# Gated linear attention and a multiplicative FFN in one kernel: another order in the steps that split x, and earlier loads of x

## Chip, cores and metric

The kernel runs on one core of a Trainium2 chip. The metric is the device time of one execution in microseconds (us). Before the change it is 479.17 us, the median of 6 runs (478.79 to 479.78).

## What is computed

```python
for t in range(S):                                   # B=4, H=8, S=768, D=48
    state = alpha[t][..., None] * state + outer(k[t], v[t])   # per batch and head
    y[t] = q[t] @ state
x = y.transpose(0, 2, 1, 3).reshape(B * S, H * D)    # 3072 x 384
out = ((x @ w1) * (x @ w2)) @ w3 @ w_out             # d_ff = 1024, d_model = 384
```

All activations are fp32. The four weights reach the kernel as 64-bit floats, read as pairs of 32-bit words, so each weight has to be converted to fp32 on the chip first.

## The kernel before

**The recurrence as chunks.** The sequence of each batch is cut into 6 chunks of 128 positions, 24 chunks in all. The main loop (L583) has one step per chunk. Step n does on TensorE (PE), in this order: `attend_state(n-1)` (L369, queries times the carried state), `scores(n)` (L349, keys times queries), `transposed(n+1)` (L309, transposes of the decayed q and k), `attend(n-1)` (L375, values times masked scores), `outer(n)` (L321, the new state), then a few pieces of the FFN's first half (L405), with `decays(n+3)` (L271 or L274, cumulative sums of the logarithms of alpha) among them. The first step of a batch has no state to carry, so L369 is missing in steps 7, 13 and 19.

**What the other engines do for it.** VectorE (DVE) masks the scores (`ms`, L352, two instructions for each chunk), multiplies q and k by their decays (L287), adds up the state (L329, L331), and takes part in all splits and conversions. ScalarE (ACT) copies the transposes out of PSUM (`qkT`, L311, two), copies the attention's output (`x`, L379, two), and does logarithms and exponentials (L256, L260, L277, L278). All PSUM tiles come from one pool of 8 banks in turn: a matmul that opens a bank waits for the instruction that read what was in it before.

**x through DRAM.** `attend` leaves its output x in a buffer of two; `store()` at the head of the next step sends it to the DRAM tensor `xd[g]` (L246). A group g is 3 chunks, 384 tokens. `load_x(g)` (L391) reads it back transposed into `xT`, of which there is one buffer, and `split_x(g)` (L393) splits it into the three parts of `x3`: ACT computes a rounded high part (L397), DVE the remainder (L398) and a third part that corrects the rounding (L399). FFN products (L405, fp32r) use all three. `x3` has one buffer in this half of the kernel, and `xT`'s next load waits for L399 of the split before.

**Which steps split x.** `begin` (L581) maps steps 4, 8, 12, 16, 20 to groups 0 to 4. At such a step the group's load is issued, after `logs`; two steps later, in steps 6, 10, 14, 18 and 22, `split_x` is called after `scores` and `transposed`, and the group's tiles are put into `fill`, from which `run` takes pieces (none in steps 6, 10, 14, 18 and 22, three, three and two in the steps after each). Groups 0 to 3 do 4 of the 8 tiles there, group 4 all 8, so the second half of w1 and w2 is first needed for group 4's later tiles, after the main loop.

**Weight conversion.** A weight block is one load (L189) and a generator: L197, L198, L201, L202 in its first stage, L204, L205, L207 in the second, L214 (ACT) in the third, L216 and L217 (DVE) in the last. `convert(1)` runs one stage. In the later steps it is called once after the split's place, and once more at the end of every third step.

**Who decides the order.** Each engine executes its own list in order. The Tile scheduler makes these lists from the traced program; `tc.issue_after(ins)` holds what is traced in the block behind `ins` on the same engine. `after_marks(...)` (L108) applies it to instructions remembered in `mark`: `("ms", n)` is the second mask, `("qkT", n)` the second copy of the transposes. SyncE (SP) issues nearly all DMAs of the main loop in one in-order queue: for each step x's store, then v, alpha, k and q of later chunks, a weight block, the store of an FFN tile (`abd`, L480). GpSimd (POOL) issues the small DMAs of the decays and, after the main loop, the later loads of x.

**After the main loop** come the FFN's other tiles (L405 with w12), the product w3 times w_out (L405 with wo), and the last projection (L405 with w3o).

Of the kernel before, what the change touches and what calls it, by code (L numbers as in the profile page):

```python
# [10 lines left out]
FP32 = mybir.dt.float32  # L11
# [5 lines left out]
ALU = mybir.AluOpType  # L17
# [3 lines left out]
P = 4096.0  # L21
# [27 lines left out]
def kernel(  # L49
# [12 lines left out]
    nc = tc.nc  # L62
# [43 lines left out]
    st, mark = {}, {}  # L106

    def after_marks(*names):  # L108
        stack = ExitStack()
        for x in names:  # L110
            stack.enter_context(tc.issue_after(mark[x]))
        return stack
# [16 lines left out]
    def load_a(n):  # L129
        if n < N:  # L130
            st["a", n] = inp.tile([C, H, D], FP32, tag="ac", name="ac")
            nc.sync.dma_start(out=st["a", n], in_=rows(alpha, n))

    def load_kq(n):
        if n >= N:
            return
        st["kq", n] = inp.tile([C, 2, H, D], FP32, tag="kq", name="kq")
        nc.sync.dma_start(out=st["kq", n][:, 0], in_=rows(k, n))
        nc.sync.dma_start(out=st["kq", n][:, 1], in_=rows(q, n))  # L139

    def load_v(n):
        if n < N:
            st["v", n] = vs[n % len(vs)]
            nc.sync.dma_start(out=st["v", n][:, :, 0:D], in_=rows(v, n))
# [81 lines left out]
    def convert(steps, ahead=3):  # L226

        for _ in range(steps):
            fetch(ahead)
            if not begun:  # L230
                return
            x = begun.popleft()
            try:
                next(x)
                begun.appendleft(x)
            except StopIteration:
                pass
# [4 lines left out]
    def store():  # L242

        while later:
            dst, src = later.popleft()
            nc.sync.dma_start(out=dst, in_=src)  # L246
# [4 lines left out]
    def logs(n):  # L251
        if n >= N:
            return
        a = st.pop(("a", n)).rearrange("p h d -> p (h d)")
        la = st["la", n] = work.tile([C, DM], FP32, tag="la", name="la")
        nc.scalar.activation(la, a, AF.Ln)  # L256
        if n >= LATE:

            t = st["la", n] = work.tile([C, 2, DM], FP32R, tag="la2", name="la2", bufs=1)
            nc.scalar.copy(t[:, 0], la)  # L260
            nc.vector.tensor_sub(t[:, 1], la, t[:, 0].bitcast(FP32))
        if n in ends:
            nc.gpsimd.dma_start(out=ends[n][2:3], in_=a[0:1])

    def decays(n):
        if n >= N:
            return
        lc = bank()[:, 0:DM]
        la = st.pop(("la", n))
        if n < LATE:  # L270
            nc.tensor.matmul(lc, utri if n % 2 else after, la, start=True, stop=True)  # L271
        else:
            for i in range(2):
                nc.tensor.matmul(lc, sums[:, n % 2], la[:, i], start=(i == 0), stop=(i == 1))  # L274

        e = st["e", n] = work.tile([C, 2, DM], FP32, tag="e", name="e", bufs=3)
        nc.scalar.activation(e[:, 0], lc, AF.Exp, scale=-1.0)  # L277
        mark["e", n] = nc.scalar.activation(e[:, 1], lc, AF.Exp).ins  # L278
        if n in ends:
            nc.gpsimd.dma_start(out=ends[n][0:1], in_=e[0:1, 0])  # L280
        if n + 1 in ends:
            nc.gpsimd.dma_start(out=ends[n + 1][1:2], in_=e[C - 1:C, 1])
        load_ends(n)
# [14 lines left out]
    def transposed(n):  # L298
        if n >= N:
            return  # L300
        qk = qks[n % 3]
        qkT = work.tile([C, 2, NP, C], FP32, tag="qkT", name="qkT")

        tp = [bank().rearrange("p (i j c) -> p i j c", i=2, j=NP) for _ in range(2)]
        for i in range(2):
            for j in range(NP):
                for half in range(2):
                    s = ds(DP * half, DP)
                    nc.tensor.transpose(tp[half][:, i, j, :], qk[s, i, 2 * j:2 * j + 2, :], ident[s, s])  # L309
        for half in range(2):  # L310
            mark["qkT", n] = nc.scalar.copy(qkT[:, :, :, ds(DP * half, DP)], tp[half]).ins  # L311
        st["qkT", n] = qkT
# [30 lines left out]
    def scores(n):  # L343
        qkT = st["qkT", n]
        sc = [bank().rearrange("p (j c) -> p j c", j=NP) for _ in range(2)]
        for j in range(NP):
            for i in range(2):
                r = ds(DP * i, D)
                nc.tensor.matmul(sc[i][:, j, :], qkT[r, 0, j, :], qkT[r, 1, j, :], start=True, stop=True)  # L349
        ms = work.tile([C, 2, NP, C], FP32, tag="ms", name="ms")  # L350
        for i in range(2):
            masked = nc.vector.tensor_tensor(ms[:, i].bitcast(I32), sc[i].bitcast(I32), keep_bc, op=ALU.bitwise_and)  # L352
        ends_of_part1[0] = mark["ms", n] = masked.ins
        st["ms", n] = ms
# [3 lines left out]
    def attend_state(n):  # L358
        qkT = st.pop(("qkT", n))

        y = [bank()[:, 0:HP * C].rearrange("p (j c) -> p j c", c=C) for _ in range(2)]
        st["y", n] = y, [(half * HP + j, i, y[i][ds(DP * half, DP), j, :])
                         for j in range(HP) for i in range(2) for half in range(2)]
        if n % NCH:
            for j, i, to in st["y", n][1]:
                r = ds(DP * i, D)
                nc.tensor.matmul(to, Ts[n % 2][r, j, :], qkT[r, 1, j, :],  # L369
                                 start=(j % HP == 0), stop=False, skip_group_check=True)  # L370
# [18 lines left out]
    def load_x(g, queue=nc.sync):  # L389
        st["xT", g] = xp.tile([C, KM, TG], FP32, tag="xT", name="xT")  # L390
        queue.dma_start(out=st["xT", g], in_=xd[g].rearrange("(k p) t -> p k t", p=C))  # L391

    def split_x(g, i):  # L393
        x = st.pop(("xT", g))
        t = tr[i].tile([C, 3, KM, TG], FP32R, tag="x3", name="x3")
        st["x3", g] = t
        nc.scalar.activation(t[:, 0], x, AF.Copy, scale=1.0 - 2.0 ** -13)  # L397
        nc.vector.tensor_sub(t[:, 1], x, t[:, 0].bitcast(FP32))  # L398
        nc.vector.scalar_tensor_tensor(t[:, 2], t[:, 0].bitcast(FP32), -1.0 - 1.0 / P, x,  # L399
                                       op0=ALU.mult, op1=ALU.add)  # L400

    def products(p, w, x, parts, n, start, stop):
        for part in parts:
# [70 lines left out]
    def gate(g, f):  # L474
        yield from (late_gate if late else early_gate)(g, f)
# [73 lines left out]
    def run(pieces):  # L549

        for _ in range(pieces):
            if not fill:
                return
            try:
                next(fill[0])
            except StopIteration:
                fill.popleft()
# [21 lines left out]


    begin = {4 + 4 * g: (g, range(FH if g < 4 else KF)) for g in range(5)}  # L581

    for n in range(N + 1):  # L583
        store()
        load_v(n + AHEAD - 1)
        load_a(n + 5)
        load_kq(n + AHEAD)
        if n:
            attend_state(n - 1)
        if n < N:  # L590
            scores(n)
        transposed(n + 1)
        if n - 2 in begin:
            g, tiles = begin[n - 2]
            split_x(g, 0)
            fill.extend(gate(g, f) for f in tiles)
        pieces = (0, 3, 3, 2)[(n - 6) % 4] if n > 5 else 0
        if n == 0:
            with after_marks(("qkT", 0)):
                logs(2)  # L600
            decays(2)
            with after_marks(("e", 2)):
                logs(3)
        early = n < 7
        behind = after_marks(("qkT", n + 1), ("qk", n + 1)) if early else ExitStack()
        if n < N - 2:
            with behind:
                convert(2 if n == 0 else 1, 2 if n == 0 else 3)
        advance(n)
        if n:  # L610
            attend(n - 1)
        outer(n)
        run(pieces > 0)
        if early:
            with after_marks(("qkT", n + 1), ("qk", n + 1)):
                convert(1)
        with after_marks(*[("ms", n)] * (n < 3)):
            decayed(n + 2)
        logs(n + 4)
        if n in begin:  # L620
            load_x(begin[n][0])
        convert(early and n > 2)
        run(pieces > 1)
        decays(n + 3)
        if n < N - 2:
            convert(early or n % 3 == 0)
        run(pieces > 2)
        if n == N - 3:
            while begun:
                convert(1)  # L630
            weights.extend(load_out(j) for j in range(KF))
            fetch(4)
# [91 lines left out]
```

## Time and profile before

| what | value |
|---|---|
| median of 6 runs | 479.17 us |
| the profiled execution | 478.79 us, span 477.0 us |
| busy: PE, DVE, ACT, POOL | 457.9, 359.6, 279.3, 73.4 us |
| granted PE clock, 60 to 187 us | 1.00 |
| 57 to 187 us: busy PE, DVE, ACT | 126.05, 110.88, 84.63 us of 130 |
| 57 to 187 us: mean share of the 16 DMA engines | 0.95, at 210 GB/s |

In this execution, by PE's first instruction, step 7 begins at 57.5 us, step 11 at 89.5, step 15 at 118.3, step 19 at 149.3, step 23 at 177.2, and the main loop has ended on PE at about 187. A row of the timeline gives the start, the duration, the engine, the line, what is written from what, and in brackets how long the engine was idle before it and what ended that. Matmuls are pipelined, so PE counts as busy while it streams; the weight loads (PEld) show the short waits better. Durations on one engine overlap by some 0.08 us, so that two masks of 0.68 us take 1.28 us together.

### The profile page before, as it was taken

What the parts mean: (1) busy time and instruction counts of PE and PEld (TensorE: products, weight loads), DVE (VectorE), ACT (ScalarE), POOL (GpSimd) and SP (SyncE); (2) the same over time, 40 slices, a digit from 0 to 9 for tenths busy, and PEclk for the clock granted to TensorE, in tenths of its full rate; (3) what the DMA queues carried; (4) which work ended last, traced back from release to release, by engine and by line L of the source; (5) the groups of instructions that cost most, each with busy time, mean ns of one, the idle gap of its engine ahead of it and who ended that gap; (6) DMA issues with size and microseconds to landing.
All of it is one profiled execution on the core that took longest, in us unless ns stands there. A gap on an engine that the chain in (4) does not pass through costs nothing.

```text
span 477.0 us, 9968 instructions
## 1 busy us (share of the span) xinstructions
PE 457.9 (96%) x3824; PEld 434.2 (91%) x3824; DVE 359.6 (75%) x582; ACT 279.3 (59%) x550; POOL 73.4 (15%) x138
## 2 busy tenths in 40 slices
PE   4898889999999999999999999999999999999996
PEld 2676679898998989999999999999999999999996
DVE  2689899997989666999998888745642876666761
ACT  4577667775767545898886666644545433333330
POOL 2322132121202310212331102202010100000000
PEclk9998799999999999999999999999999999999999
DMA  9999999999999864557775332122105965555511
GB/s 171 183 216 214 241 194 203 245 178 245 194 236 212 214 197 135 188 172 230 240 226 177 136 124 101 57 77 88 45 34 161 263 180 173 164 170 172 175 51 49
DMA packets 153584, 80.29 MB, mean 168 GB/s; under 512 B 104481, under 2 KB 145569, under 8 KB 153537
## 3 DMA queue, kind: packets, MB, share of 16 engines
q1 hardware_dynamic: 148016, 65.22, 56.7%
q0 software_dynamic: 5520, 14.43, 9.2%
q8 instruction: 30, 0.49, 0.4%
q14 instruction: 18, 0.14, 0.1%
HBM read 57.58 MB, written 22.06 MB: 167 GB/s over the span
## 4 chain that ended last, share of the span: by engine, by line
PE 84%; DVE 5%; DMA 5%; ACT 3%; issue 1%; SPq 1%; ACTq 0%; DVEq 0%
PE bank L405 70%; PE bank L349 3%; PE bank L375 3%; DMA raw<-in_moe_w_dram 2%; PE bank L309 2%; PE bank L369 1%; PE bank L507 1%; DMA ac<-in_alpha_dram 1%; DMA abd<-ab 1%; DVE ms L352 1%; PE bank L271 1%; PE bank L321 1%; PE bank L274 1%; SPq L139 1%; ACT qkT L311 1%
## 5 line engine op out<-in xcount | busy, mean ns | idle before, releaser
L405 PE MATMUL bank<-x,w 128*128 128x384 f32 x1152 | 211.2, 338 | 0.3 <-DVE x L399 0.3
L405 PEld LDWEIGHTS bank<-x,w 128*128 128x128 f32 x1152 | 200.2, 188 | 1.9 <-issue 1.1
L405 PE MATMUL bank<-w3o,ab 128*128 128x384 f32 x576 | 100.2, 336 | 0.0
L405 PEld LDWEIGHTS bank<-w3o,ab 128*128 128x128 f32 x576 | 99.9, 188 | 0.0
L430 ACT ACTIVATE bank<-bank 128x384 f32<-128x384 f32 x98 | 46.7, 477 | 42.8 <-PE bank L405 42.5
L414 ACT ACTIVATE t<-bank 128x384 f32<-128x384 f32 x62 | 30.4, 492 | 61.2 <-PE bank L405 61.0
L480 POOL DMA_DIRECT2D abd<-ab x46 | 26.8, 583 | 133.0 <-DVE ab L466 125.1
L466 DVE TENSOR_TENSOR ab<-bank,r 128x384 f32<-128x384 f32 x45 | 24.9, 554 | 23.5 <-ACT bank L430 17.8
L536 DVE TENSOR_TENSOR ab<-abl,ab 128x1024 fp32r<-128x1024 f32 x24 | 29.4, 1224 | 13.5 <-ACT ab L535 13.5
L535 ACT ACTIVATE ab<-abl 128x1024 fp32r<-128x1024 f32 x24 | 25.5, 1061 | 20.5 <-PE bank L405 18.9
L405 PE MATMUL bank<-wo,w3T 128*128 128x384 f32 x192 | 35.9, 334 | 0.0
L349 PEld LDWEIGHTS bank<-qkT 48*128 48x128 f32 x384 | 26.4, 205 | 9.4 <-issue 4.5
L352 DVE TENSOR_TENSOR ms<-bank,keep 128x512 int32<-128x512 int32 x48 | 31.2, 686 | 4.3 <-PE bank L349 4.3
L349 PE MATMUL bank<-qkT 48*128 48x128 f32 x384 | 31.5, 306 | 2.3 <-DVE ms L352 1.3
L311 ACT COPY qkT<-bank 128x512 f32<-128x512 f32 x48 | 26.0, 587 | 13.1 <-PE bank L309 13.1
L405 PEld LDWEIGHTS bank<-wo,w3T 128*128 128x128 f32 x192 | 33.5, 188 | 0.0
L416 DVE SCALAR_TENSOR_TENSOR o<-bank,t 128x384 f32<-128x384 f32 x24 | 13.4, 558 | 24.1 <-issue 15.2
L202 ACT ACTIVATE power<-power,rebias 128x512 uint32<-128x512 uint32 (+1 forms) x36 | 25.0, 698 | 9.6 <-DVE power L201 9.3
L287 DVE TENSOR_TENSOR qk<-kq,e 128x768 f32<-128x768 f32 x24 | 22.9, 954 | 8.7 <-ACT e L278 8.7
L537 DVE SCALAR_TENSOR_TENSOR ab<-ab,abl 128x1024 fp32r<-128x1024 f32 x24 | 29.2, 1218 | 0.0
L416 DVE SCALAR_TENSOR_TENSOR r<-bank,t 128x384 f32<-128x384 f32 x38 | 21.1, 554 | 10.5 <-PE bank L405 5.9
L375 PE MATMUL bank<-ms,v 128*64 128x128 f32 x384 | 28.7, 293 | 0.0
(75 smaller groups left out, 571.5 us busy)
## 6 DMA issues: line engine op xcount, KB each, us to landing
raw<-in_moe_w_dram SPq DMA_DIRECT2D x28, 512.0 KB, 5.3
abl<-abd SPq DMA_DIRECT2D x24, 512.0 KB, 4.4
abd<-ab POOLq DMA_DIRECT2D x46, 192.0 KB, 3.0
xT<-xd POOLq DMA_DIRECT2D x9, 576.0 KB, 4.5
ac<-in_alpha_dram SPq DMA_DIRECT2D x24, 192.0 KB, 5.0
kq<-in_k_dram SPq DMA_DIRECT2D x24, 192.0 KB, 5.3
kq<-in_q_dram SPq DMA_DIRECT2D x24, 192.0 KB, 4.4
v<-in_v_dram SPq DMA_DIRECT2D x24, 192.0 KB, 4.8
```

Source lines behind the costliest of these rows:

```text
L311: mark["qkT", n] = nc.scalar.copy(qkT[:, :, :, ds(DP * half, DP)], tp[half]).ins
L349: nc.tensor.matmul(sc[i][:, j, :], qkT[r, 0, j, :], qkT[r, 1, j, :], start=True, stop=True)
L352: masked = nc.vector.tensor_tensor(ms[:, i].bitcast(I32), sc[i].bitcast(I32), keep_bc, op=ALU.bitwise_and)
L375: nc.tensor.matmul(to, vc[:, 2 * j + i, :], ms[:, i, j, :], start=(n % NCH == 0 and j % HP == 0), stop=(j % HP == HP - 1), skip_group_chec ...
L405: nc.tensor.matmul(p, w[part][i], x[part][i], start=start and part == parts[0] and i == 0, stop=stop and part == parts[-1] and i == n - 1, ...
L414: nc.scalar.activation(t, p1, AF.Copy, scale=(1.0 + 1.0 / P) * scale)
L416: nc.vector.scalar_tensor_tensor(to, p2, scale, t, op0=ALU.mult, op1=ALU.add)
L430: nc.scalar.activation(p, p, AF.Copy, scale=1.0 + 1.0 / P)
L480: (nc.gpsimd if late else nc.sync).dma_start(out=abd[g][:, f, :], in_=ab)
L535: nc.scalar.activation(t[:, 0], ab, AF.Copy, scale=1.0 - 2.0 ** -13)
L536: nc.vector.tensor_sub(t[:, 1], ab, t[:, 0].bitcast(FP32))
L537: nc.vector.scalar_tensor_tensor(t[:, 2], t[:, 0].bitcast(FP32), -1.0 - 1.0 / P, ab, op0=ALU.mult, op1=ALU.add)
```

## The change

In the five steps with a split of x, three things are reordered, and three of the five loads of x are called one step earlier.

- `split_x` is held behind the step's masks (on DVE) and behind its copies of the transposes (on ACT).
- The conversion stage that is traced next in that step is held behind L399, the last instruction of the split, which is marked `"x3"` for this. (DVE alone carries the mark, so ACT's part is held only by its data.)
- `load_x` of groups 2, 3 and 4 is called in steps 11, 15 and 19 instead of 12, 16 and 20; the calls for groups 0 and 1 stay.

```diff
@@ split_x
-        nc.vector.scalar_tensor_tensor(t[:, 2], t[:, 0].bitcast(FP32), -1.0 - 1.0 / P, x,
-                                       op0=ALU.mult, op1=ALU.add)
+        mark["x3"] = nc.vector.scalar_tensor_tensor(t[:, 2], t[:, 0].bitcast(FP32), -1.0 - 1.0 / P, x,
+                                                    op0=ALU.mult, op1=ALU.add).ins
@@ before the main loop
     begin = {4 + 4 * g: (g, range(FH if g < 4 else KF)) for g in range(5)}
+    loads = {4: 0, 8: 1, 11: 2, 15: 3, 19: 4}
@@ the main loop
-            split_x(g, 0)
+            with after_marks(("ms", n), ("qkT", n + 1)):
+                split_x(g, 0)
...
-        behind = after_marks(("qkT", n + 1), ("qk", n + 1)) if early else ExitStack()
+        behind = after_marks(*[("qkT", n + 1), ("qk", n + 1)] * early, *["x3"] * (n - 2 in begin))
...
-        if n in begin:
-            load_x(begin[n][0])
+        if n in loads:
+            load_x(loads[n])
```

## The prediction

> **What bounds the kernel now.** I read the page first, then who PE waited for, then the timeline around each split, at last the order in which the changed program's instructions stand on each engine.
>
> ```profile
> PE 84%; DVE 5%; DMA 5%; ACT 3%; issue 1%; SPq 1%; ACTq 0%; DVEq 0%
> ```
>
> By the page PE is busy for 96% of the span (457.9 us), DVE for 75%, and PE carries 84% of the chain that ended last. From 57 us on the chain is PE almost without a break, so this change can win only what PE still waits for in steps with a split, and every us that PE gains or loses there reaches the end. PE's waits from 0 to 260 us:
>
> ```profile
> PE bank L271 <- ACT la L256: 8.3, 4, 4.4
> PE bank L309 <- DVE qk L287: 3.2, 2, 2.0
> PE bank L349 <- DVE ms L352: 1.3, 3, 0.7
> PE bank L349 <- ACT la L260: 1.0, 1, 1.0
> PE bank L274 <- ACT la L260: 1.0, 1, 1.0
> PE bank L405 <- DVE x L399: 0.3, 1, 0.3
> ```
>
> The first two lie before 60 us. Down to step 8 the change leaves the order on every engine as it was, so the waits around the first split (L309 at 59.8, L399 at 63.5, L274 at 66.9, 2.4 us together) stay. What it can reach is about 2 us: the 1.0 us of L349 in step 19, one of 0.35 us in step 23, and two or three of 0.3 us in steps 11 and 15 that only the weight loads show. The timeline at step 19, then at step 23:
>
> ```profile
> 147.14 1.35 DVE L398 TENSOR_TENSOR x<-xT,x 128x1152 fp32r<-128x1152 f32 x1
> ...
> 148.41 1.28 DVE L352 TENSOR_TENSOR ms<-bank,keep 128x512 int32<-128x512 int32 x2
> ...
> 149.25 1.16 PE L349 MATMUL bank<-qkT 48*128 48x128 f32 x16 [1.03 <-ACT la L260]
> ```
>
> ```profile
> 177.38 1.28 DVE L352 TENSOR_TENSOR ms<-bank,keep 128x512 int32<-128x512 int32 x2
> ...
> 178.21 1.16 PE L349 MATMUL bank<-qkT 48*128 48x128 f32 x16 [0.35 <-DVE ms L352]
> ```
>
> Both times the split (in step 23 L398 and L399, from 174.84 to 177.46) stands ahead of the masks on DVE, and the next scores wait for a bank that the first mask frees. (At 149.25 the profile names L260, but L349 waits on the mask, which ends just as late.)
>
> **Step 11 (group 1).** On DVE the changed order takes L216 and L217 out from in front of step 10's masks: 2 x 0.6 us. It hardly helps: DVE's L261 and L287 wait there for ACT's L260 and L278, which end at 87.3 and 87.6, and the masks can move from 89.20 to 89.1 only. L397 already stood behind L311. I take -0.1 (bounds 0 and -0.3, the wait in the weight loads).
>
> **Step 19 (group 3).** L398 leaves the place in front of the masks (148.41 - 147.14 = 1.27 us), and so does a conversion stage (L217, 0.6). The masks come at 146.5 to 147.1 and are through before PE asks. PE's L274 pair begins at 147.60 and takes 0.35 to 0.45, so the scores begin at 148.05 instead of 149.25: -1.2 us. L397 moves behind both L311; L379 comes at 148.3 instead of 147.3, which is before the bank that it frees is wanted (149.7). What is late next: the split and the conversion that follow. L399 ends at 151.0; a whole conversion (L198, L201, L204, L205, L207, L216, L217: 2 x 0.34 + 5 x 0.61 = 3.7 us of DVE) now stands in steps 19 and 20 in place of 14 to 16. Adding DVE's list up from 148.4, the L416 that PE's tile at 160.1 needs ends at 160.0, and the masks of step 20 end 0.2 to 0.5 before their banks are asked for. I give 0.1 back: -1.1 (bounds -1.2 and -0.3, the latter if these margins fail by 0.3 us three times).
>
> **Step 23 (group 4).** The masks come first, at 174.3 where PE has finished the scores, and step 23's scores start when L369 is done (177.19 + 0.6 = 177.79) instead of 178.21: -0.4. L398 and L399 follow behind L331; L399 ends 0.3 us before the third part of x3 is multiplied. Bounds -0.4 and 0.
>
> **The load of x and what it is moved past, step 15 (group 2).** The masks of step 14 come at 116.4 to 116.7 instead of 117.47, since the conversion and L453 (which waited for a DMA until 116.99) no longer stand before them; PE's 0.31 us wait for them goes. But this is the timeline there:
>
> ```profile
> 110.18 0.80 SPq L189 DMA_DIRECT2D raw<-in_moe_w_dram  x1
> 111.08 0.39 SPq L480 DMA_DIRECT2D abd<-ab  x1
> 111.51 0.43 SPq L391 DMA_DIRECT2D xT<-xd  x1
> ...
> 116.41 0.68 ACT L197 ACTIVATE rest<-raw 128x512 f32<-128x512 uint32 x1 [0.94 <-DMA raw<-in_moe_w_dram]
> ...
> 116.99 1.06 ACT L311 COPY qkT<-bank 128x512 f32<-128x512 f32 x2
> ...
> 118.41 1.17 ACT L397 ACTIVATE x<-xT 128x1152 fp32r<-128x1152 f32 x1 [0.36 <-DMA xT<-xd]
> ```
>
> ACT waits for the weight block, and behind it in ACT's list stand the copies L311, which the scores of step 15 need. In the changed order L197 still stands there. The load of xT is taken from behind this block and put, on SP, at 103.66: ahead of one `abd` store, both x stores, v, alpha, k, q and the block. It waits there for L399 of group 1, done at 93.3, so SP isn't held; but the DMA engines are full (share 0.97 from 105 to 110 us, 1.13 in the next 5), and all that is behind it lands later by d.
>
> How large is d? The weight block is there at 116.41, the `abd` store at 116.99, xT at 118.41: in the order of issue, xT 1.42 us behind its predecessor. The other end: median 5.8 us from issue to landing for xT, 3.5 for `abd`, 2.3 apart. Take 0.15 off for the idle 3% of 5 us: d is 1.3 to 2.15, and I take 1.6, nearer to the row of this very load. The Trainium skill speaks against the move here (DMA: Bandwidth & Descriptors, "Queues, rings and completion order"): a queue's descriptors are consumed on each engine in the order of its ring, so all 576 KB go first. The landings above agree. The same page's fit ("Anatomy of one DMA", for loads by the software path) gives a moving part of bytes/436e3, an estimate of 589,824/436,000 = 1.35 us, d = 1.2. If the DMAs merely shared the engines, d would be near 0.
>
> With d, L197 starts at 116.41 + d, L311 0.58 later, L397 at 117.98 + d (xT is long there), L277 1.08 after it, L379 0.39 later at 119.45 + d; PE's second transposes, which before went on at 120.67, 0.42 after L379's start, go on at 119.87 + d. That is d - 0.8 against before: +0.8 us with d = 1.6; +0.4 by the fit; with d under 0.8 nothing is won, since L379 itself waits for a DMA (0.30 us before 120.25), an x store that is not sooner. Without this term the whole sum would be -1.6.
>
> **The other moved loads and queues.** Group 3's load goes past an `abd` store, two x stores, v, alpha, k, q and an `abd` store (from 139.57 to about 132.1), group 4's past `abd`, x stores, v and `abd` (160.93 to 157.9); the L399 that each waits for has ended by 124 and 151. What is delayed by d: the x store that L379 at 140.4 needs, the alpha for L256 at 140.9, the tile buffer for L453 at 138.7. They cost ACT and DVE up to 1 us, and PE nothing by my sum (its masks come 0.4 us ahead of need). 0, bounds 0 and +0.4. No instruction moves on POOL; its load for group 5 waits for group 4's L399, now at 179.5 instead of 177.5, and lands by 187 at the worst, ahead of its L397 (190.4). The deferred conversions of w1 and w2 end at about 169, wanted after 187. Both cost nothing.
>
> **Sum.** -0.1 - 1.1 - 0.4 + 0.8 = -0.8 us against the profiled execution's 478.79 (span 477.0 and 1.8 around it). That execution is 0.4 under the median of the six; on the median 479.17 - 0.8 = 478.4.
>
> **Rivals.** (1) *As summed*: 478.4, by its bounds 477.8 to 479.4. 55%. (2) *The weight block is not late*: d under 0.8, because the DMA engines' share counts waiting too and they can take 576 KB more. For it: xT's 1.42 is near the page's bare moving time. Then -0.1 - 1.1 - 0.4 = -1.6, 477.5. 20%. (3) *The moved load makes it slower*: xT costs the queue more than 1.42, and ACT stands still in front of L311. The sign turns at d = 2.4. With xT's slowest landing (6.9 us, less the 3.5 of `abd`) d = 3.3, step 15 loses 2.5: +0.9, and with the 0.4 of the other loads 480.5. Against it: in that landing the block was ahead of xT. 15%. (4) *DVE becomes the bound*: the reordering does what it says, but the split and the deferred conversion (6 us of DVE in a row from step 19) make PE wait for L416 and the masks in steps 20 and 21; step 19's gain is given back: 0.3, 479.4. DVE is full only in stretches (25.38 us busy of the 37 from 150). 10%.
>
> **Numbers.** I predict 478.4. About 0.2%, 1 us, is what a measurement of this kernel can tell from no change. Case 1 lies to two fifths beyond it on the fast side (0.22), otherwise within it (0.33); case 2 is faster (0.20); case 3 is slower (0.10) or within (0.05); case 4 is within. Faster 0.42, same 0.48, slower 0.10. The range takes in cases 1, 4, most of 2 and the near part of 3: 477.3 to 479.8.
>
> **What would show it.** Right: L349 of step 19 without a wait; no L352 wait in step 23; ACT's L197 in step 15 idle for 2 us or more on the weight block, and L311 right behind it. The waits of L309, L399 and L274 from 59 to 67 us are as before. Wrong: L197 idle for about 1 us as now (case 2); new waits of PE for L416 or L352 from 155 to 170 us (case 4); waits on x stores or alpha in steps 16 and 17 that reach PE.

## The result, and the profile after

The changed kernel takes 478.33 us (median of 34 runs) where the kernel before takes 479.74 us (71 runs): a ratio of 0.9969, 95% interval 0.9955 to 0.9983, which is 1.5 us less (0.8 to 2.2). A second comparison (e8 below) gave 0.9969 again, 0.9945 to 0.9992. The kernel before compared with itself (e10) gave 1.0007, 0.9991 to 1.0023, so the gain is real and small. The forecast of 478.4 was close in time, in part by luck; most of what follows is about how differently it came about.

The profiled execution takes 478.55 us, span 476.8. The page's chain by engine, then PE's waits from 0 to 260 us (in all, times, longest):

```profile
PE 81%; DVE 6%; DMA 4%; SPq 3%; ACT 3%; issue 2%; DVEq 0%; ACTq 0%
```

```profile
PE bank L271 <- ACT la L256: 7.8, 3, 4.3
PE bank L309 <- DVE qk L287: 3.8, 3, 2.0
PE bank L349 <- ACT qkT L311: 2.2, 1, 2.2
PE bank L274 <- ACT la L260: 1.0, 1, 1.0
PE bank L349 <- ACT t L414: 1.0, 1, 1.0
PE bank L405 <- DVE x L399: 0.3, 1, 0.3
PE bank L309 <- ACT x L379: 0.2, 1, 0.2
PE bank L405 <- ACT e L278: 0.2, 1, 0.2
```

PE's share of the chain has fallen from 84 to 81%, and SP's issue has risen to 3%. The waits of L349 for the masks (L352) and for L260 in steps 19 and 23 are gone. In their place stands one of the same size, L349 for ACT's L414, which is in step 20. (L271, L274, L399, the first L309 and the wait for L311 lie before 70 us.) The timeline, steps 19 and 20 (L369 opens step 20 on PE, L375 comes behind its scores and transposes):

```profile
145.65 1.28 DVE L352 TENSOR_TENSOR ms<-bank,keep 128x512 int32<-128x512 int32 x2
...
147.35 1.16 PE L349 MATMUL bank<-qkT 48*128 48x128 f32 x16
...
147.59 1.36 DVE L398 TENSOR_TENSOR x<-xT,x 128x1152 fp32r<-128x1152 f32 x1 [0.32 <-ACT x L397]
...
152.62 0.54 ACT L414 ACTIVATE t<-bank 128x384 f32<-128x384 f32 x1
155.94 0.67 PE L369 MATMUL bank<-qkT,T 48*64 48x128 f32 x16
156.12 0.52 ACT L256 ACTIVATE la<-ac 128x384 f32<-128x384 f32 x1 [2.96 <-DMA ac<-in_alpha_dram]
156.55 0.61 ACT L214 ACTIVATE w<-mant 128x512 fp32r<-128x512 f32 x1
157.07 0.47 ACT L414 ACTIVATE t<-bank 128x384 f32<-128x384 f32 x1
...
157.59 1.16 PE L349 MATMUL bank<-qkT 48*128 48x128 f32 x16 [0.98 <-ACT t L414]
...
159.78 1.09 PE L375 MATMUL bank<-ms,v 128*64 128x128 f32 x16
```

The same two lines before the change:

```profile
157.54 0.67 PE L369 MATMUL bank<-qkT,T 48*64 48x128 f32 x16
...
159.73 1.09 PE L375 MATMUL bank<-ms,v 128*64 128x128 f32 x16
```

Step 19 does what was forecast: masks first, scores at 147.35 without a wait, the split behind them. Then ACT stands still for 2.96 us in front of L256, whose alpha has not landed. Behind L256 stand L214 (which the hold on the conversion has put there) and the L414 that empties the bank PE needs next. PE reaches step 20 1.60 us sooner than before (155.94 against 157.54; step 8 began 0.45 sooner), and by L375 nothing is left of it (159.78 against 159.73): 1.05 us goes in front of the scores, 0.60 in the transposes behind them, which wait for L278 and the next L414, both behind the late L256. Steps 15 and 23:

```profile
116.58 0.69 ACT L197 ACTIVATE rest<-raw 128x512 f32<-128x512 uint32 x1 [1.46 <-DMA raw<-in_moe_w_dram]
117.18 1.06 ACT L311 COPY qkT<-bank 128x512 f32<-128x512 f32 x2
118.12 1.18 ACT L397 ACTIVATE x<-xT 128x1152 fp32r<-128x1152 f32 x1
...
119.55 0.66 ACT L379 COPY x<-bank 128x256 f32<-128x256 f32 x2
...
119.99 0.71 PE L309 MATMUL bank<-ident,qk 64*128 64x64 f32 x15 [0.23 <-ACT x L379]
...
175.40 1.29 DVE L352 TENSOR_TENSOR ms<-bank,keep 128x512 int32<-128x512 int32 x2 [0.46 <-PE bank L349]
...
177.87 1.16 PE L349 MATMUL bank<-qkT 48*128 48x128 f32 x16
...
178.06 1.36 DVE L398 TENSOR_TENSOR x<-xT,x 128x1152 fp32r<-128x1152 f32 x1 [0.24 <-ACT x L397]
```

In step 15 xT no longer holds L397, and the weight block (L197) is not 1.6 us late: it lands within 0.2 us of where it did (0.45 us later, counted from the scores of step 14). PE's second transposes go on at 119.99 (120.67 before). In step 23 the 0.35 us wait is gone.

### The profile page after: what moved, and what is told of

The parts are those of the page before. It is cut to its first block, busy times and chain, and to the rows that moved or that the text cites. A ratio compares the mean times of both kernels' runs of the same rounds, so it can differ in the third digit from the quotient of the medians.

```text
span 476.8 us, 9973 instructions
## 1 busy us (share of the span) xinstructions
PE 456.2 (96%) x3824; PEld 433.4 (91%) x3824; DVE 359.3 (75%) x582; ACT 278.0 (58%) x550; POOL 74.5 (16%) x138
## 4 chain that ended last, share of the span: by engine, by line
PE 81%; DVE 6%; DMA 4%; SPq 3%; ACT 3%; issue 2%; DVEq 0%; ACTq 0%
PE bank L405 68%; PE bank L375 3%; PE bank L349 3%; DMA raw<-in_moe_w_dram 2%; DMA ac<-in_alpha_dram 2%; PE bank L369 2%; PE bank L309 2%; SPq L139 1%; PE bank L507 1%; DVE ms L352 1%; PE bank L321 1%; DVE qk L287 1%; PE bank L274 1%; DVE mant L207 1%; DVE power L205 1%
## 5 line engine op out<-in xcount | busy, mean ns | idle before, releaser
L414 ACT ACTIVATE t<-bank 128x384 f32<-128x384 f32 x62 | 30.4, 492 | 57.5 <-PE bank L405 57.3
L480 POOL DMA_DIRECT2D abd<-ab x46 | 28.2, 613 | 131.7 <-DVE ab L466 124.0
L536 DVE TENSOR_TENSOR ab<-abl,ab 128x1024 fp32r<-128x1024 f32 x24 | 29.4, 1224 | 13.4 <-ACT ab L535 13.4
L349 PEld LDWEIGHTS bank<-qkT 48*128 48x128 f32 x384 | 25.8, 203 | 9.5 <-issue 3.6
L349 PE MATMUL bank<-qkT 48*128 48x128 f32 x384 | 30.8, 303 | 3.2 <-ACT qkT L311 2.2
L352 DVE TENSOR_TENSOR ms<-bank,keep 128x512 int32<-128x512 int32 x48 | 31.2, 684 | 2.4 <-PE bank L349 2.4
L311 ACT COPY qkT<-bank 128x512 f32<-128x512 f32 x48 | 26.0, 586 | 11.7 <-PE bank L309 11.6
L416 DVE SCALAR_TENSOR_TENSOR o<-bank,t 128x384 f32<-128x384 f32 x24 | 13.4, 558 | 23.7 <-issue 15.2
L197 ACT ACTIVATE rest<-raw 128x512 f32<-128x512 uint32 (+1 forms) x36 | 23.1, 646 | 10.6 <-DMA raw<-in_moe_w_dram 10.5
L375 PE MATMUL bank<-ms,v 128*64 128x128 f32 x384 | 29.2, 295 | 0.0
L287 DVE TENSOR_TENSOR qk<-kq,e 128x768 f32<-128x768 f32 x24 | 23.0, 960 | 8.0 <-ACT e L278 8.0
```

The lines of the kernel that those rows point to most:

```text
L287: mark["qk", n] = nc.vector.tensor_mul(qks[n % 3][:, :, :, 0:D], st.pop(("kq", n)), st.pop(("e", n)).rearrange("p i (h d) -> p i h d", h=H ...
L375: nc.tensor.matmul(to, vc[:, 2 * j + i, :], ms[:, i, j, :], start=(n % NCH == 0 and j % HP == 0), stop=(j % HP == HP - 1), skip_group_chec ...
L414: nc.scalar.activation(t, p1, AF.Copy, scale=(1.0 + 1.0 / P) * scale)
L480: (nc.gpsimd if late else nc.sync).dma_start(out=abd[g][:, f, :], in_=ab)
L536: nc.vector.tensor_sub(t[:, 1], ab, t[:, 0].bitcast(FP32))
```

## How the profiles were compared

Runs of one kernel spread over 4 to 7 us, so one profile is one draw. The table gives, for the profiled execution of each kernel of this study, PE's time from the first L349 of one step to that of another, read from the timeline; from the scores of step 23 to the end of the span it is an almost constant 298.7 to 299.0 us. (Where an expectation below names a stretch to the last scores, it counts these scores too, 0.9 us more than the last column.)

| kernel | profiled, us | step 8 begins | 14 to 16 | 18 to 22 | 22 to 23 | 8 to 23 |
|---|---|---|---|---|---|---|
| before | 478.79 | 69.63 | 14.04 | 29.59 | 4.08 | 108.58 |
| before, second (e10) | 478.36 | 69.57 | 13.47 | 29.68 | 4.08 | 108.21 |
| before, third (e11) | 483.42 | 71.20 | 14.79 | 31.98 | 4.08 | 111.69 |
| before, fourth (e12) | 479.70 | 70.60 | 13.39 | 30.17 | 4.08 | 108.52 |
| changed | 478.55 | 69.18 | 13.61 | 30.47 | 3.66 | 108.69 |
| changed, second (e8) | 479.86 | 69.88 | 13.12 | 31.77 | 3.66 | 109.24 |
| e1 loads as before | 478.74 | 69.96 | 13.12 | 30.75 | 3.66 | 108.23 |
| e2 sooner loads alone | 480.69 | 69.02 | 14.63 | 30.75 | 4.08 | 111.10 |
| e3 conversion not held | 477.91 | 70.68 | 13.41 | 28.67 | 3.66 | 106.70 |
| e4 group 2 loaded as before | 479.40 | 68.98 | 16.93 | 28.51 | 3.66 | 109.86 |
| e5 every alpha first | 480.62 | 72.02 | 14.86 | 28.84 | 3.66 | 108.07 |
| e6 hold alone | 481.10 | 70.85 | 15.03 | 29.88 | 4.08 | 109.70 |
| e7 an extra transfer | 478.99 | 69.09 | 13.20 | 30.45 | 3.66 | 109.40 |
| e9 last alpha first | 478.57 | 69.12 | 13.65 | 30.46 | 3.66 | 108.93 |

Down to step 8 the instructions stand in the same order in all of them, and yet step 8 begins anywhere from 69.0 to 72.0 us.

## The experiments

The times, each against the kernel before on the same chip:

| kernel | ratio | 95% interval |
|---|---|---|
| e1 masks first and hold, loads as before | 0.9964 | 0.9945 to 0.9982 |
| e2 sooner loads alone | 1.0072 | 1.0044 to 1.0100 |
| e3 masks first and loads, no hold | 0.9992 | 0.9972 to 1.0012 |
| e4 the change, group 2 loaded as before | 0.9962 | 0.9944 to 0.9979 |
| e5 the change, every alpha ahead of the stores | 0.9987 | 0.9967 to 1.0007 |
| e6 hold alone | 0.9985 | 0.9964 to 1.0005 |
| e7 the change and an extra 576 KB | 0.9968 | 0.9949 to 0.9987 |
| e8 the change again | 0.9969 | 0.9945 to 0.9992 |
| e9 the change, last alpha ahead of the stores | 0.9974 | 0.9952 to 0.9997 |
| e10 before again | 1.0007 | 0.9991 to 1.0023 |

Three theories stood at the start. Theory 1: masks and copies first is what gains, and the sooner loads are worth little. Theory 2: the sooner loads gain. Theory 3: the hold on the conversion is what moves the time.

**e1, the order without the loads.**

```diff
-    loads = {4: 0, 8: 1, 11: 2, 15: 3, 19: 4}
+    loads = {4: 0, 8: 1, 12: 2, 16: 3, 20: 4}
```

> The change without the sooner loads (groups 2 to 4 loaded where the kernel before loads them). Theory 1 (masks and copies first is what gains, in steps 19 and 23; the sooner loads are worth between -0.4 and +0.4 us): about 1.5 us below the kernel before; L349 of step 19 without a wait, step 19 about 1.1 us shorter on PE; step 15 waits for xT or its copy as before. Theory 2 (the sooner loads gain): within 0.3 us of the kernel before, and step 19 keeps its 1 us wait. Step 20's wait for alpha (2.9 us of idle ACT before L256 in the changed kernel's profile, 1 us of it reaching PE) comes by theory 1 only if the group load stands ahead of alpha in the queue; without it L256 of step 20 should idle under 1 us and PE not wait for L414 at 157 us.

Measured: 0.9964. The whole gain is there without the loads, so theory 2 falls. The side expectation on step 20 fell as well: PE waits 1.35 us for L414 at 157.84 although no group load stands ahead of alpha. The sooner load does not cause that wait:

```profile
157.84 1.16 PE L349 MATMUL bank<-qkT 48*128 48x128 f32 x16 [1.35 <-ACT t L414]
```

**e2, the loads without the order.**

```diff
+    loads = {4: 0, 8: 1, 11: 2, 15: 3, 19: 4}
-        if n in begin:
-            load_x(begin[n][0])
+        if n in loads:
+            load_x(loads[n])
```

> The kernel before with the sooner loads of groups 2 to 4 alone, order of masks, split and conversion as before. Theory 1: 0 to +0.5 us against the kernel before; L349 of step 19 still waits about 1 us, L352 of step 23 still holds PE 0.35 us. Theory 2: about 1.5 us below the kernel before. Theory 3 (the deferred conversion is what moves the time): 0, no change anywhere.

Measured: 1.0072, 3.5 us slower, which no theory expected. The changed lists fit a scheduler that places an instruction by when it expects its data: with xT sooner it put the split further forward. Step 19:

```profile
146.59 1.35 DVE L398 TENSOR_TENSOR x<-xT,x 128x1152 fp32r<-128x1152 f32 x1
...
148.33 1.28 DVE L352 TENSOR_TENSOR ms<-bank,keep 128x512 int32<-128x512 int32 x2
...
149.53 1.34 DVE L399 SCALAR_TENSOR_TENSOR x<-x,xT 128x1152 fp32r<-128x1152 f32 x1
...
151.06 0.94 DVE L287 TENSOR_TENSOR qk<-kq,e 128x768 f32<-128x768 f32 x1
...
152.15 0.71 PE L309 MATMUL bank<-ident,qk 64*128 64x64 f32 x16 [1.33 <-DVE qk L287]
```

L399 now stands ahead of L287, and the transposes that L287 feeds wait 1.33 us; step 15 has the same wait of 1.21 us. With the marks of the change neither wait is there. This execution (480.69 us) is one of the kernel's fastest; its median is 484.39. The mean granted clock of its runs was 0.983, against 0.987 for the kernel before beside it. One stretch at half clock (last section) is 0.0036 of the span, so by an estimate the runs have about one such stretch more, behind the two waits, and this trace shows none after 60 us.

**e3, the conversion free again.**

```diff
-        behind = after_marks(*[("qkT", n + 1), ("qk", n + 1)] * early, *["x3"] * (n - 2 in begin))
+        behind = after_marks(*[("qkT", n + 1), ("qk", n + 1)] * early, )
```

> The change with the conversion no longer held behind the third part of x3 (masks and copies first and the sooner loads stay). Theory 1: as the changed kernel in step 19 if the conversion does not slip ahead of the masks again (at least half of the 1.1 us), and in step 20 no L214 stands between L256 and L414 on ACT, so a late alpha costs PE at most what L256 itself is late; 0.8 to 1.8 us below the kernel before. Theory 3: the gain is gone, within 0.3 us of the kernel before.

Measured: 0.9992, where theory 1 wanted 0.9963 to 0.9983 and theory 3 up to 0.3 us either way. By time theory 3 is the nearer. Its profile looks different: the shortest stretch of all (106.70 us), with step 20 free of the alpha wait: alpha landed at 153.3, and no L214 stands between L256 and L414. The first alone would do, so this profile doesn't show what the second is worth. That execution, 477.91 us, lies 2 us under this kernel's median, so its trace isn't the typical one.

**e6, the hold alone.** The kernel before with the `"x3"` mark and the hold only.

```diff
-        behind = after_marks(("qkT", n + 1), ("qk", n + 1)) if early else ExitStack()
+        behind = after_marks(*[("qkT", n + 1), ("qk", n + 1)] * early, *["x3"] * (n - 2 in begin))
```

> The kernel before with one part of the change alone: the conversion held behind the third part of x3. Masks, copies and split stand as before and the loads are as before. After the first four runs (order with hold 0.9964, without the hold 0.9992, loads alone 1.0072) two theories are left. Theory 1 (masks and copies first is what gains, the hold only keeps the conversion from slipping back in front of the masks): within 0.5 us of the kernel before, step 19's L349 still waits. Theory 3 (the hold itself is what gains): 1.0 to 1.5 us below the kernel before.

Measured: 0.9985, 0.7 us less with an interval that reaches no change. Its profile keeps step 19's wait, at 0.60 us instead of 1.03 or more, and step 23's 0.35. So neither part was seen to gain by itself: masks first with the sooner loads and no hold is worth 0.0008 (e3), the hold alone 0.0015, masks first with the hold 0.0036 (e1). The three intervals overlap, and masks first without the hold and without the sooner loads was not run; since sooner loads can cost time where nothing holds their consumers (e2), e3 may show the masks too small. Which part gains, or whether it takes both, stays open.

**e4, group 2's load back.**

```diff
-    loads = {4: 0, 8: 1, 11: 2, 15: 3, 19: 4}
+    loads = {4: 0, 8: 1, 12: 2, 15: 3, 19: 4}
```

> The change with group 2 loaded in step 12 again, as before (groups 3 and 4 stay sooner). If moving this load ahead of the weight block delays the block by d = 0.45 us (what the profile of the changed kernel shows), then step 15 loses the 0.4 us that it gained: PE goes on after the second transposes at about 120.4 us in place of 120.0, and the time is 0 to 0.5 us above the changed kernel. If the block's delay was larger (1.6 us as forecast), the time falls by up to 0.8 us instead, and ACT's L197 starts 1 us or more earlier.

Measured: 0.9962, as the change. The profile is the most telling one for the load. ACT's timeline in steps 15 and 20:

```profile
119.48 1.16 ACT L397 ACTIVATE x<-xT 128x1152 fp32r<-128x1152 f32 x1 [1.78 <-DMA xT<-xd]
...
156.15 0.53 ACT L256 ACTIVATE la<-ac 128x384 f32<-128x384 f32 x1 [0.59 <-DMA ac<-in_alpha_dram]
```

At its old place xT landed at 119.46, 3.4 us behind the weight block, and steps 14 to 16 took 16.93 us, of which about 1.6 belong to the clock (last section). In step 20 alpha landed at 156.1 as in the changed kernel, but PE was 2.9 us later by then, so ACT waited 0.59 us and PE not at all.

**e7, the suspected cost twice.** The output is not touched; the transfer is work added.

```diff
+                nc.sync.dma_start(out=extra.rearrange("(k p) t -> p k t", p=C),
+                                  in_=xd[0].rearrange("(k p) t -> p k t", p=C))
```

> The change with a second transfer of 576 KB (rows of the same length, from one buffer in memory to another; nothing reads it) right behind the sooner load of group 2, so that the suspected cost d is there twice. The planner, which counts the transfer, puts L197 of step 15 behind L397, L277 and L278 in ACT's list, so what is read is when the weight block lands. If 576 KB delay what follows by the forecast's 1.6 us or more, the block lands at about 118.2 us and the alpha behind it late as well, 0.5 to 2 us on the time. If d is the 0.45 us that the changed kernel's profile showed, or less, the block lands before 117.2 and the time stays within 0.5 us of the changed kernel.

Measured: 0.9968, as the change. The extra transfer landed 1.45 us behind xT (111.74 against 110.29), and the weight block at 118.61. By landing the larger d is right, though the block was late at its issue (113.50 against 110.75 in the changed kernel) and landed 5.11 us after it, sooner than the 5.81 there. By time it costs nothing that can be seen. L197 now stands behind L397, L277 and L278, on which PE depends in step 15 (14 to 16: 13.20 us), which would explain it; its steps 8 to 14 took 46.31 us, though, where the changed kernel's took 45.16 and 44.91. Step 19's mask wait came back there (1.48 us), with the changed lists.

**e8, the changed kernel again.**

> The changed kernel itself, beside the others on the same chip, and a second profile of it. 0.9955 to 0.9983 of the kernel before as in the first measurement. Step 19 without the L349 wait and step 23 without the L352 wait in any execution. Step 15's wait for the weight block and step 20's wait for alpha hang on DMA landings, which differ by 1 to 2 us between the profiles so far: if they belong to the change, L256 of step 20 idles for about 3 us again; if to the execution, either can be gone.

The second profile has neither L349's wait in step 19 nor L352's in step 23, and the same alpha wait in step 20:

```profile
155.93 0.52 ACT L256 ACTIVATE la<-ac 128x384 f32<-128x384 f32 x1 [3.35 <-DMA ac<-in_alpha_dram]
...
157.40 1.16 PE L349 MATMUL bank<-qkT 48*128 48x128 f32 x16 [1.04 <-ACT t L414]
```

So that wait belongs to the change. What followed it is the clock (last section).

**e5 and e9, alpha sooner.** e5 issues each alpha from step 12 on ahead of its step's x stores and v, e9 only the last one, for step 20.

```diff
     for n in range(N + 1):
+        if n == 18: load_a(n + 5)
         store()
         load_v(n + AHEAD - 1)
-        load_a(n + 5)
+        if not (n == 18): load_a(n + 5)
```

> The change with alpha's load put ahead of the step's x stores and v on the queue from step 12 on (aimed at the one new wait in the changed kernel's profile: L256 of step 20 idle 2.96 us, PE held 1.2 us at 157.6). If alpha's landing is what step 20 gives back in most executions: L256 of step 20 idles under 1 us, PE does not wait for L414 at 157 us, and the time is 0.5 to 1.5 us below the changed kernel. If that wait belonged to one execution only, or if L256, which now stands ahead of L414 and L379 in ACT's list in steps 13 to 17, holds those: 0 to +1.5 us against the changed kernel.

> The change with one load moved: the last alpha (issued for step 20's L256) stands ahead of its step's x stores and v on the queue; L256 then stands one place sooner, ahead of L379 and L414, in ACT's list of step 20, and nothing else moves. All three profiles with the changed order in steps 19 and 20 and alpha at its old place lose 1.2 to 1.6 us to this wait at 157 us. If that loss is real in most executions: alpha lands at 153 to 154 us, L256 idles 1.5 us or less, L414 no longer holds L349 of step 20, and the time is 0.8 to 1.5 us below the changed kernel (0.994 of the kernel before). If PE's wait only moves (L379 or L414 late behind L256): within 0.4 us of the changed kernel.

Measured: 0.9987 and 0.9974, neither better than the change. In e5 step 20 is clean (18 to 22: 28.84 us), but L256 now stands ahead of L278 in ACT's list of step 15, and PE waits for that:

```profile
122.10 0.52 ACT L256 ACTIVATE la<-ac 128x384 f32<-128x384 f32 x1
...
123.28 0.51 ACT L278 ACTIVATE e<-bank 128x384 f32<-128x384 f32 x1
...
123.84 0.71 PE L309 MATMUL bank<-ident,qk 64*128 64x64 f32 x15 [1.44 <-ACT e L278]
```

In e9 alpha is in time, and the wait moves to the transfer that it was moved past:

```profile
151.84 0.54 ACT L256 ACTIVATE la<-ac 128x384 f32<-128x384 f32 x1
154.82 0.65 ACT L379 COPY x<-bank 128x256 f32<-128x256 f32 x2 [2.45 <-DMA xd<-x]
...
155.25 0.79 PE L405 MATMUL bank<-x,w 128*128 128x384 f32 x3 [1.73 <-ACT x L379]
```

L379 needs the buffer that the x store frees. Steps 18 to 22 take 30.46 us, as with the change. This fits a step 20 in which not one load is late but SP's stream as a whole, and PE runs into it with what step 19 gains; one profile of e9 is all that speaks for it.

**e10, e11, e12, the kernel before three more times.**

> The kernel before itself, as a second profile and as a measure of the comparison: ratio 1.000, within 0.2%. If the 1.5 us that the change gains in timed runs although its two profiles show steps 8 to 23 no shorter than the first profile of before comes from waits that the first profile of before happened not to show, this profile has them: L309 of step 15 waits for L379 by about 1.2 us (as in the two other profiles with group 2 loaded in step 12 that showed it), or granted clock below 1 after 85 us; and step 19's L349 wait of about 1 us again. If not, steps 8 to 23 take the same 108.6 us as in the first profile.

> The kernel before, a third profile. Open is why timed runs have the change 1.5 us ahead while its profiles do not: in the two profiles of before the scores of step 8 begin at 69.6 us and the stretch from there to the last scores takes 109.1 to 109.5 us, in the two of the changed kernel 69.2 and 69.9 us, 109.6 and 110.1 us. If before is in most executions slower than its two profiles, and in the steps of the change, this one takes 110.5 us or more for the stretch (a wait of L309 for L379 in step 15, a lower granted clock after step 19's wait). If it is the start-up, whose instruction order is the same in all kernels here, step 8 begins at 70.5 us or later and the stretch takes 109.3 us. If neither, the time is 478.3 to 479 again, and the gain of the timed runs is not found in profiles.

> The kernel before, a fourth profile, read like the third: stretch of 110.5 us or more (the steps of the change), step 8 at 70.5 us or later (the start-up), or neither.

PE's scores of step 19 in the three, one profile each:

```profile
148.86 1.16 PE L349 MATMUL bank<-qkT 48*128 48x128 f32 x16 [1.16 <-DVE ms L352]
```

```profile
152.47 1.83 PE L349 MATMUL bank<-qkT 48*128 48x128 f32 x16 [1.96 <-DVE ms L352]
```

```profile
150.14 1.16 PE L349 MATMUL bank<-qkT 48*128 48x128 f32 x16 [1.59 <-DVE ms L352]
```

With the first profile's 1.03, step 19's wait is 1.0 to 2.0 us, mean 1.4. e10 showed neither of what was sought, e12 the later start-up only, e11 both: step 8 at 71.20 us, and a stretch of 111.69 us with L309's wait of 0.90 us for L379 in step 15, the 1.96 us in step 19, and the clock after it.

## Why the prediction came out near, and where it failed

The sum was 0.8 us less; measured was 1.5 (0.8 to 2.2). That 478.4 meets 478.33 is in part luck: the kernel before took 479.74 in this measurement, 0.6 more than the 479.17 that the forecast started from, and in the profiles two terms fail in opposite directions, the loss of 0.8 in step 15 that did not come and the 0.1 of step 20 that became 1.65. One sum was added wrongly: the upper bounds of all terms together are 0 - 0.3 + 0 + 1.35 + 0.4, which is 480.6 and not 479.4.

**Step 19, -1.1: right in its place, and undersized for before.** The wait of 1.03 us is gone in all profiles that have masks first, loads sooner or not, except e7. In before it is 1.4 us on average.

**"I give 0.1 back" in steps 20 and 21: the step that failed.** I added up DVE's list and took its margins as the limit; the rival that expected step 20 to give the gain back also named DVE. In the changed kernel's two profiles DVE was in time (in e6, with the hold but the split still ahead of the masks, PE waits 0.38 us for L352 in step 20). What PE meets is alpha on SP's queue, behind which ACT's L256 holds L214 and L414: 1.65 us given back in step 20 where I had 0.1. Alpha itself lands no later than in before (156.09 and 155.91 us, against 154.27 to 157.36 in the four); it is PE that comes sooner. Steps 18 to 22 take 30.47 and 31.77 us where before takes 29.59 to 31.98. In e3, e4 and e5, where alpha is not late for PE, they take 28.5 to 28.8: the gain I forecast, and where it goes. I had weighed the alpha of 140.9 us, not that of step 20, and of the instructions deferred I had counted DVE's, not ACT's L214.

**Step 15, +0.8: the loss did not come, a mis-sized term.** d, by which what is issued behind the load of xT lands later, was 1.6 in the sum. From the scores of step 14 to the block's landing it is 1.76, 0.81, 1.59 and 0.59 us in the four profiles of before, mean 1.19; 2.22 and 1.36 in the two of the change and 2.27 in e9 (the same up to there), mean 1.95. So d is about 0.8, which the prediction itself named as the point from which nothing is lost. It also comes another way than forecast. The block's own time from issue to landing has not grown: 5.6 to 6.4 us in the seven profiles with this load at its old place, 5.1 to 5.9 in the seven with it sooner. But the block is issued later: 4.1 to 5.5 us ahead of the scores of step 14 in before, 3.1 to 3.7 in the change, e8 and e9. What has grown is the issue of a load of k ahead of the block, on SP, which the prediction took to be free ("SP isn't held"): 0.54 to 0.81 us in the first seven, 1.43 to 3.37 in the others. In before and in the change:

```profile
108.36 0.54 SPq L138 DMA_DIRECT2D kq<-in_k_dram  x1
```

```profile
108.08 1.82 SPq L138 DMA_DIRECT2D kq<-in_k_dram  x1
```

Why SP is held there was not tested. Steps 14 to 16 take 13.4 to 14.8 us in before, and 13.1 to 13.65 in the change, e8 and e9. By means (13.92 and 13.37, of the change and e8) that is 0.5 less instead of 0.8 more, but it can't be put down to the sooner load: with the load at its old place and the new order e1 takes 13.12 and e4 16.93. In the timed runs it doesn't show either: e1 and e4 equal the change within their intervals.

**Step 23, -0.4: right.** 4.08 us from step 22 to 23 in every kernel with the old order of masks, 3.66 in every one with the new.

**Step 11, -0.1, and the other loads, 0: right within what can be seen.** Steps 10 to 12 take 13.1 us in before, 13.28 and 13.03 in the change.

**What stays open.** By the profiles' means steps 8 to 23 take 109.25 us in before (four) and 108.97 in the change (two): 0.3 less, where timed runs have 1.5. Step 8 begins 0.7 earlier in the two than in the four, but the order up to there is the same and the scatter 3 us, so I don't count this as the change's. A reading that fits: a run in which PE comes late to step 20 doesn't meet the alpha wait and keeps about 2 us (e4's steps 18 to 22 are 1.1 us below the shortest of before, step 23 adds 0.4, step 15 perhaps 0.5); a run in which PE comes early keeps nothing. 1.5 us would be the mixture. e4 shows one such case by chance; to show the mixture, many profiles of each kernel would be needed. It is argued, not shown. The granted clock is not the source of the gain: its mean over the runs is 0.987 (the change) and 0.986 (e8), against 0.987 to 0.988 for the kernel before in three sets of runs.

## What to carry to other kernels

Moving work off the place where PE waits lets PE run ahead; before counting the gain, ask which transfer it meets next, and which instructions of every engine stand behind the one that waits for it. A sooner load is not neutral under a scheduler that places instructions by when their data arrive: without a mark that holds its consumer it cost 3.5 us here, with one nothing. It can also hold up the queue that issues it, and so what is issued behind it. Where runs of one kernel spread by more than the gain, take several profiles of the kernel before, since one draw of a landing or a wait can be half of another.

## What the hardware showed unasked

After some of PE's short waits the granted clock fell to half. Stretches of 1 us in e8 (after the 1.04 us wait at 157.40) and in e11 (after the 1.96 us at 152.47); the last three columns are the granted clock, the DMA share and GB/s:

```profile
159.00:160.00 1.00, 1.00 (x17) 0.88 (x19) 1.00 (x3) 0.26 (x1) 0.00 (x0) 0.69 1.46 216
160.00:161.00 1.00, 1.00 (x12) 1.00 (x12) 1.00 (x3) 0.81 (x2) 0.00 (x0) 0.50 0.89 90
161.00:162.00 1.00, 1.00 (x18) 1.00 (x16) 1.00 (x2) 0.61 (x2) 0.00 (x0) 0.50 0.78 240
162.00:163.00 1.00, 1.00 (x13) 0.91 (x11) 1.00 (x3) 0.13 (x1) 0.14 (x1) 0.61 1.05 389
```

```profile
152.00:153.00 1.00, 0.53 (x7) 0.56 (x9) 1.00 (x3) 0.64 (x2) 1.00 (x2) 0.89 0.85 231
153.00:154.00 1.00, 1.00 (x13) 1.00 (x12) 1.00 (x1) 0.00 (x0) 0.79 (x2) 0.50 0.67 133
154.00:155.00 1.00, 1.00 (x20) 0.96 (x17) 1.00 (x4) 0.00 (x0) 0.00 (x0) 0.50 1.36 208
155.00:156.00 1.00, 1.00 (x13) 0.92 (x12) 1.00 (x2) 0.88 (x2) 0.00 (x0) 0.50 1.43 140
156.00:157.00 1.00, 1.00 (x26) 1.00 (x24) 0.99 (x2) 0.67 (x3) 0.00 (x0) 0.90 1.45 160
```

Counting 0.31/0.5 of the first stretch as half-rate, then 1, 1 and 0.39/0.5, this is 3.4 us in e8; in e11 and in e4 (from 122 us, after step 15's wait) it is 3.4 us too. It costs PE 1.6 us: step 20 takes 11.08 us in e8 where the changed kernel's first profile has 9.50. The waits of 1.73 us in e9, 1.59 in e12, 1.48 in e7 and 1.35 in e1 had no such consequence. The Trainium skill (TensorE: Matmul & The Clock Gate, Part 1) describes a free-running window of about 3.4 us by whose activity the clock is gated to half, and puts the drop after an idle window. The length and the half agree, and so does the free run: within one execution all half-rate stretches begin on one grid of 3.413 us (in e4 at 29.91, 50.39 and 122.07), so they start 0.3 to 2.0 us after the end of the wait. But PE was never idle for a window here. In the window of the grid before the drop it was busy for 0.42 (e11), 0.66 (e8) and 0.67 (e4) of the time, and no drop followed on 0.50 in e9, 0.58 in e5 and 0.60 in e1. Neither the length of the wait nor this share tells which waits are punished; a wait of 1 to 2 us costs itself and, in some executions, 1.6 us more.
